# Running the first layer of a fused attention and two-layer kernel in two passes of eight feature chunks

## The chip, the cores and the metric

The kernel runs on one core of a Trainium2 chip. The metric is the device time of one launch in microseconds (us). Engines are named as the profile names them: PE is TensorE (matmuls), PEld its weight loads, DVE is VectorE, ACT is ScalarE, POOL is GpSimd, SP is the engine whose queue issues every DMA of this kernel.

## What is computed

Three steps follow each other on 3072 tokens: an attention over chunks of 32 queries with a short window, then `h * cos(h)` between two products, then a maximum of three products and a last product. The weights come as float64.

```python
for c in range(768 // 32):                       # 4 batches, 8 heads of 64
    k_full = concat([mem_k, k[c*32-16 : c*32+40]])   # 8 memory keys, 16 left, 8 right
    a = softmax(q_c @ k_full.T / 8)
    out_c = a @ v_full
x = out.reshape(3072, 512)
h = x @ w_in                                     # 512 -> 2048
x = (h * cos(h)) @ w_out                         # 2048 -> 512
h = maximum(maximum(x @ w1, x @ w2), x @ w3)     # 512 -> 768
y = h @ w_out2                                   # 768 -> 512
```

## The kernel before

**Blocks, slots, products.** The 3072 tokens are 8 blocks of 384 (`NBLK`, `N`). The 2048 features of the first layer are 16 chunks of 128 (`FA`). One block with one chunk is a *slot*; slots are numbered through all blocks, so before the change slot 16 is block 1, chunk 0. Every product is done in three passes, because each operand is split into a high and a low float32r part. A slot has a first product, `p1` (12 matmuls into `h`, L319), a *chain* on the other engines, and a second product, `p2` (12 matmuls into four accumulators `acc`, L348). `LOOK = 2`: the program writes `p2` of slot s-2 behind `p1` of slot s.

**The chain of a slot** makes `g = h cos h`: ScalarE `ki` (L328), VectorE L330 and L331, ScalarE sine (L333), VectorE L335, ScalarE high part of `g` (L337), GpSimd low part of `g` (L338). So a slot takes three VectorE instructions.

**Weight decoding.** A weight tile (128x512 float64, 512 KB) is loaded, has its exponent rebased (`w_exp`: one instruction on GpSimd, L154, or ScalarE, L152, and one on ScalarE, L156), takes two integer instructions on VectorE (`w_bits`: L161 and L163, called its first and its second half here), is copied to its high part by ScalarE (`w_hi`, L169), and gets its low part by a subtraction (`w_lo`, L174) on GpSimd for the first layer, and in turns on VectorE and GpSimd for the second. The first layer has 32 tiles, the second 24. A loaded tile sits in a staging tile until its low part is made. Before the change there are 9 staging tiles in the first layer, 6 in the second. `Decode` takes up two tiles in a slot (`RATE`) in the first layer, about 1.1 in the second.

**Attention.** A block has 3 *duos* of 128 queries. The tables `FIRST`, `SECOND` and `STEADY` say after which slot a step of a later duo is written: S scores on TensorE (L208), with two additions of the mask and a maximum on VectorE (L223, L228) and a subtraction on GpSimd (L229); E one exponential for a block (L233); N a sum, an addition and a reciprocal on VectorE (L238, L239, L240) and a multiplication on GpSimd (L241); T transposes (L250), evicted half by ScalarE, half by VectorE (L254); V values (L266), evicted by ScalarE and VectorE (L270, L271). The attention of block 0 is done ahead of the slots.

**Stages.** A start with loads, the attention of block 0 and the first two tiles; 16 slots of block 0 beside the other 30 tiles and the attention of block 1; six blocks with attention alone; block 7, without attention, beside the 24 tiles of the second layer; then the second layer, 48 steps of `b3` (L395) and `b4` (L416). The output of the first layer goes to DRAM (`x2d`) and comes back block by block (`b_dma`, `b_conv`).

**What sets the order.** The program is written as above, but the order in which instructions stand in each engine's queue is made when the program is built, by a list scheduler of the kernel language. It may put an instruction ahead of earlier written ones as soon as its tiles have a free buffer and its inputs exist. Each engine then takes its queue strictly in that order.

Of the kernel before, what the change touches and what calls it, by code (L numbers as in the profile page):

```python
# [41 lines left out]
LOOK = 2  # slots that a second product waits for its operand  # L42

# Emission plan. A slot is one of the FA feature chunks of a token block; it names the steps of the attention of later
# duos that follow its products: S scores, E exponential of a whole block, N normalization, T transposes, V values.
# [21 lines left out]
def attn_moe_kernel(ctx, tc, qT, kT, vw, w_in, w_out, w3, w2o, out):  # L67
# [56 lines left out]
    stage_state = {}  # L124

    def stage_open(keys, n_raw, n_tmp):
        """Staging tiles; the first n_raw of them hold the last weights in the end."""
        tiles = [wp.tile([128, 512, 2], I32, tag="w", name=f"raw{i}") for i in range(n_raw)]
        tiles += [tmp["pool"].tile([128, 512, 2], I32, name=f"wst{i}", bufs=1) for i in range(n_tmp)]
# [545 lines left out]
```

## Time and profile before

| | before |
|---|---|
| time, median of 3 runs | 1098.11 us (1097.15 to 1098.32) |
| span of the profiled execution | 1098.8 us |
| TensorE busy, matmuls | 1056.0 us, 96% |
| VectorE busy | 513.2 us, 47% |
| ScalarE busy | 433.6 us, 39% |
| GpSimd busy | 316.1 us, 29% |

The span is taken from the first to the last instruction of one profiled execution; it is 0.7 us above the median of the timed runs. Shares are means over stages that differ: the stages have to be read one by one.

### The profile page before, as it was taken

The numbers are of one execution on the slowest core, as the hardware profiler recorded it, in microseconds if no ns is written. First come the engines' busy times: TensorE is split into PE (matmuls) and PEld (weight loads), VectorE is DVE, ScalarE is ACT, GpSimd is POOL, SyncE is SP. The second block draws the span as 40 slices with busy tenths as digits, with TensorE's granted clock in tenths as the row PEclk, the third lists the DMA queues.
The fourth block names the chain that finished last, engine by engine and source line by source line (L and its number), as shares of the span: only waits on it lengthen the run. The fifth ranks groups of instructions, "written<-read, shape, count | busy, mean of one in ns | idle before, by whom it ended". The sixth has DMA issues, their size and how long they took to land.

```text
span 1098.8 us, 17081 instructions
## 1 busy us (share of the span) xinstructions
PE 1056.0 (96%) x6989; PEld 1003.9 (91%) x6989; DVE 513.2 (47%) x913; ACT 433.6 (39%) x811; POOL 316.1 (29%) x267
## 2 busy tenths in 40 slices
PE   8768899999999999999999988999999999999998
PEld 5667899999999999999999887999999999999997
DVE  5999856546346355454433998312221221222121
ACT  5667645535445335435444887211111121211111
POOL 2887635324224224233222445210101010101000
PEclk8989999999999999999999989999999999999999
DMA  9744213011111012101101662101101000100000
GB/s 287 248 150 134 83 63 97 30 65 59 30 51 58 30 52 72 44 23 30 44 16 39 226 204 78 58 5 53 30 29 30 29 29 30 58 1 30 1 30 29
DMA packets 28111, 72.94 MB, mean 66 GB/s; under 512 B 3200, under 2 KB 7296, under 8 KB 28032
## 3 DMA queue, kind: packets, MB, share of 16 engines
q1 hardware_dynamic: 28032, 71.84, 20.2%
q8 instruction: 55, 0.90, 0.3%
q14 instruction: 24, 0.20, 0.1%
HBM read 59.24 MB, written 12.58 MB: 65 GB/s over the span
## 4 chain that ended last, share of the span: by engine, by line
PE 80%; DVE 10%; issue 4%; ACT 2%; DMA 2%; POOL 1%; SPq 0%; DVEq 0%; POOLq 0%; ACTq 0%
PE h L395 27%; PE acc L348 19%; PE h L319 18%; PE acc L416 9%; PE s L208 3%; PE s L266 2%; DVE raw L161 2%; PE s L250 2%; DVE ki L331 2%; DVE wst L161 2%; DVE raw L163 1%; DVE wst L163 1%; DVE ki L330 1%; DVE ki L335 1%; DMA wst<-in_w_in_dram 1%
## 5 line engine op out<-in xcount | busy, mean ns | idle before, releaser
L319 PE MATMUL h<-x,w 128*128 128x384 f32 x1536 | 296.9, 341 | 20.2 <-DVE ki L335 15.8
L348 PE MATMUL acc<-g,w 128*128 128x384 f32 x1536 | 298.2, 341 | 12.3 <-POOL g L338 10.6
L395 PE MATMUL h<-x,w 128*128 128x384 f32 x1728 | 308.2, 335 | 0.0
L395 PEld LDWEIGHTS h<-x,w 128*128 128x128 f32 x1728 | 302.0, 188 | 4.0
L319 PEld LDWEIGHTS h<-x,w 128*128 128x128 f32 x1536 | 272.3, 191 | 25.6 <-DVE ki L335 17.9
L348 PEld LDWEIGHTS acc<-g,w 128*128 128x128 f32 x1536 | 268.2, 190 | 17.7 <-POOL g L338 13.2
L338 POOL TENSOR_TENSOR g<-ki,g 128x384 fp32r<-128x384 f32 x128 | 136.7, 1068 | 323.4 <-ACT g L337 269.1
L330 DVE SCALAR_TENSOR_TENSOR ki<-h,ki 128x384 f32<-128x384 f32 x128 | 70.9, 554 | 166.7 <-ACT ki L328 166.7
L402 DVE TENSOR_TENSOR r<-h,r 128x384 f32<-128x384 f32 x48 | 26.7, 557 | 210.3 <-PE h L395 210.3
L333 ACT ACTIVATE ki<-ki,pio 128x384 f32<-128x384 f32 x128 | 78.9, 616 | 106.3 <-DVE ki L331 106.0
L377 POOL TENSOR_TENSOR x<-xs,x 128x384 fp32r<-128x384 f32 x31 | 33.8, 1118 | 273.8 <-ACT x L376 273.8
L416 PE MATMUL acc<-w,g 128*128 128x512 f32 x432 | 107.3, 393 | 0.0
L328 ACT ACTIVATE ki<-h 128x384 int32<-128x384 f32 x128 | 62.3, 487 | 109.7 <-PE h L319 109.5
L335 DVE TENSOR_TENSOR ki<-h,ki 128x384 f32<-128x384 f32 x128 | 70.5, 551 | 54.6 <-ACT ki L333 54.4
L337 ACT ACTIVATE g<-ki 128x384 fp32r<-128x384 f32 x128 | 67.1, 525 | 72.2 <-DVE ki L335 72.1
L405 ACT ACTIVATE g<-r 128x384 fp32r<-128x384 f32 x48 | 25.1, 522 | 176.5 <-DVE r L403 176.5
L416 PEld LDWEIGHTS acc<-w,g 128*128 128x128 f32 x432 | 80.4, 188 | 14.7
L401 ACT ACTIVATE r<-h 128x384 f32<-128x384 f32 x48 | 23.6, 492 | 130.4 <-PE h L395 130.3
L331 DVE TENSOR_SCALAR ki<-ki 128x384 f32<-128x384 f32 x128 | 61.0, 477 | 2.7
L403 DVE TENSOR_TENSOR r<-h,r 128x384 f32<-128x384 f32 x48 | 26.7, 557 | 69.4 <-PE h L395 69.4
L208 PEld LDWEIGHTS s<-k,q 64*64 64x64 f32 x768 | 34.4, 137 | 8.7 <-issue 6.4
L406 DVE TENSOR_TENSOR g<-r,g 128x384 fp32r<-128x384 f32 x48 | 27.4, 571 | 31.1 <-ACT g L405 31.1
(72 smaller groups left out, 775.6 us busy)
## 6 DMA issues: line engine op xcount, KB each, us to landing
v<-in_vw_dram SPq DMA_DIRECT2D x24, 384.0 KB, 3.4
wst<-in_w_dram SPq DMA_DIRECT2D x18, 512.0 KB, 3.8
k<-in_kT_dram SPq DMA_DIRECT2D x24, 320.0 KB, 3.4
q<-in_qT_dram SPq DMA_DIRECT2D x24, 256.0 KB, 2.8
x2d<-x SPq DMA_DIRECT2D x32, 192.0 KB, 1.9
xs<-x2d SPq DMA_DIRECT2D x16, 384.0 KB, 3.1
out_dram<-ost SPq DMA_DIRECT2D x24, 256.0 KB, 2.0
raw<-in_w_out_dram SPq DMA_DIRECT2D x11, 512.0 KB, 5.8
```

Source lines behind the costliest of these rows:

```text
L208: PE.matmul(p[p0:p0 + 64, hh, :], lhsT=q[p0:p0 + 64, t, hh, :], rhs=k[p0:p0 + 64, hh, QU * t:QU * t + KU], start=first, stop=first or hh == 3)
L319: PE.matmul(h, lhsT=w[:, a, 128 * k:128 * k + 128], rhs=x[:, b, k, :], start=(n == 0), stop=(n == 11))
L328: ACT.activation(out=ki, in_=h, func=AF.Copy, scale=INV2PI, bias=0.25)
L330: DVE.scalar_tensor_tensor(c, h, INV2PI, ki, op0=ALU.mult, op1=ALU.subtract)
L331: DVE.tensor_scalar(c, c, -0.75, 0.25, op0=ALU.max, op1=ALU.min)
L333: ACT.activation(out=c, in_=c, func=AF.Sin, scale=2 * math.pi, bias=pio2)
L335: DVE.tensor_tensor(c, h, c, op=ALU.mult)
L337: ACT.activation(out=g[:, 0, :], in_=c, func=AF.Copy)
L338: POOL.tensor_tensor(g[:, 1, :], c, g[:, 0, :].bitcast(F32), op=ALU.subtract)
L348: PE.matmul(acc[j][m][:, :N], lhsT=w[:, a, 128 * m:128 * m + 128], rhs=g[:, b, :], start=(f == 0 and n == 0), stop=(f == FA - 1 and n == 2))
L395: PE.matmul(h, lhsT=w[:, a, 128 * k:128 * k + 128], rhs=x[:, b, k, :], start=(n == 0), stop=(n == 11))
L416: PE.matmul(o[m], lhsT=g[:, a, 128 * m:128 * m + 128], rhs=w[:, b, :], start=(f == 0 and n == 0), stop=(f == FB - 1 and n == 2))
```

## The change

Block and chunk change places in part. The first pass runs chunks 0 to 7 over all eight blocks, the second pass chunks 8 to 15 over all eight blocks (`slots`). So slot 8 is now block 1, chunk 0, and a block has 8 slots in a pass. Everything else follows from that:

- All attention lies in the first pass, 3 duos in 8 slots. `SECOND` also writes the scores of the next block a block early, and `X` the exponential two blocks ahead.
- `x` of every block is stored to DRAM (`x_store`, 1.5 MB) and loaded again for the second pass (`x_load`).
- Each pass leaves its own sums: `x2d` is double, `b_dma` loads both, `b_conv` adds them with one VectorE instruction for each half (128x768).
- There are no staging tiles: a loaded weight tile takes a buffer of the pool `wp` (32 buffers), like decoded weights. `live` counts them as the program is written, and `load` stops at 8 tiles ahead, or when fewer than 3 buffers are left.
- `goal` sets how many tiles are to be taken up by a slot: 2 for a slot up to the first 16, the other 16 spread over the rest of the first pass, 3 in 10 slots of the second layer's in the second pass, and 2 for a slot in its last block.

```diff
-FIRST = {0: "S0", 1: "S1", 2: "S2", 3: "E", 5: "N0", 6: "N1 T0", 7: "V0", 9: "T1", 10: "V1", 11: "N2", 12: "T2", 13: "V2"}
-STEADY = {1: "E", 3: "S3", 4: "N0 N1 T0", 6: "S4 S5", 7: "N2 V0 T1", 11: "V1", 13: "T2", 14: "V2"}
+F1 = 8
+FIRST = {0: "S0", 1: "S1", 2: "S2 E", 4: "N0 N1 N2", 5: "T0", 6: "V0 T1 V1", 7: "T2 V2"}
+STEADY = {0: "N0 N1 S3", 1: "N2", 2: "T0 S4", 3: "V0 T1", 4: "V1 S5", 5: "T2 V2", 7: "X"}
...
-NRAW, NTMP, NTMPB = 7, 2, 6
-RATE, RATEB = 2, 1.1
+NW, NAHEAD = 32, 8
+RATE = 2
...
-        t = stage(key)
+        t = wp.tile([128, 512, 2], I32, tag="w", name="raw")
+        live[0] += 1
...
+    def x_store(j):
+        SP.dma_start(out=xd[j], in_=xT[j].bitcast(F32))
+
+    def x_load(j):
+        x = xT[1, j] = xp.tile([128, 2, 4, N], F32R, tag="x", name="x")
+        SP.dma_start(out=x.bitcast(F32), in_=xd[j])
...
-        x, t = xT[NBLK + j], xs.pop((j, g))
+        x, (t, u) = xT[NBLK + j], xs.pop((j, g))
+        DVE.tensor_tensor(t, t, u, op=ALU.add)
...
+    keysA = keys_of(0, F1) + keys_of(F1, FA)
...
-            while n > 0 and self.nl < len(self.keys) and stage_state["prev"][self.keys[self.nl]] < self.ns:
+            while n > 0 and self.nl < len(self.keys) and self.nl - self.ns < NAHEAD and live[0] + 3 <= NW:
...
+    slots = [(0, j, f) for j in range(NBLK) for f in range(F1)]
+    slots += [(1, j, f) for j in range(NBLK) for f in range(F1, FA)]
+    total, half = len(slots), NBLK * F1
+
+    def goal(s):
+        if dec.keys is keysB:
+            return (s - half) * 3 // 10 if s < total - FA + F1 else dec.nb + 2
+        lead = 2 + RATE * (s + 1)
+        return lead if lead <= 2 * F1 else 2 * F1 + (s - F1 + 1) * 2 * (FA - F1) // (half - F1 - 4)
...
-        decoding = s < FA + 2 or j == NBLK - 1
-        if decoding:
-            dec.begin(RATE if s < FA + 2 else max(0, min(2, int(RATEB * (f + 1)) - dec.nb)))
+        dec.begin(max(0, min(2, goal(s) - dec.nb)))
```

The order of two queues moves with it. First VectorE, where the decoding of the first layer ends. Before, these are the last tiles (in the staging tiles `wst0` and `wst1`) and the slots behind them; L161 and L163 are the two halves, L330, L331 and L335 the chain:

```order
L161 SCALAR_TENSOR_TENSOR wst0_106<-wst0_106 128x512
L163 SCALAR_TENSOR_TENSOR wst0_106<-wst0_106 128x512
L161 SCALAR_TENSOR_TENSOR wst1_107<-wst1_107 128x512
L163 SCALAR_TENSOR_TENSOR wst1_107<-wst1_107 128x512
L330 SCALAR_TENSOR_TENSOR ki_1336<-h_1323,ki_1336 128x384
L331 TENSOR_SCALAR ki_1336<-ki_1336 128x384
L335 TENSOR_TENSOR ki_1336<-h_1323,ki_1336 128x384
L330 SCALAR_TENSOR_TENSOR ki_1380<-h_1367,ki_1380 128x384
L331 TENSOR_SCALAR ki_1380<-ki_1380 128x384
L335 TENSOR_TENSOR ki_1380<-h_1367,ki_1380 128x384
```

In the changed program (whose line numbers differ: L149 and L151 are the halves, L335, L336 and L340 the chain, L215 and L220 the mask and maximum of a duo, L246 and L264 evictions) this is VectorE in slot 14, that is block 1, chunk 6. `raw_4107` and `raw_4147` are tiles 31 and 32 of the first layer, which the program writes in slots 56 and 57:

```order
L335 SCALAR_TENSOR_TENSOR ki_1495<-h_1482,ki_1495 128x384
L336 TENSOR_SCALAR ki_1495<-ki_1495 128x384
L264 TENSOR_TENSOR x_1435<-s_1508,x_1435 128x4x128
L340 TENSOR_TENSOR ki_1495<-h_1482,ki_1495 128x384
L149 SCALAR_TENSOR_TENSOR raw_4107<-raw_4107 128x512
L215 TENSOR_TENSOR sm_1271<-s_1541,maskb_86 128x384
L151 SCALAR_TENSOR_TENSOR raw_4107<-raw_4107 128x512
L215 TENSOR_TENSOR sm_1271<-s_1542,maskb_86 128x384
L149 SCALAR_TENSOR_TENSOR raw_4147<-raw_4147 128x512
L220 TENSOR_REDUCE mx_1565<-sm_1271 128x8
L246 COPY pt_1568<-s_1575 96x512
L151 SCALAR_TENSOR_TENSOR raw_4147<-raw_4147 128x512
```

So in VectorE's queue all 32 tiles of the first layer are decoded by slot 14 in the changed program, as by slot 13 before; between them now stands the attention of two blocks.

Second TensorE's queue around the fifth `p1`. Before it goes on in turn (`h` is a `p1`, four rows of `acc` a `p2`); these are `p1` of slot 4, `p2` of slot 2, `p1` of slot 5, `p2` of slot 3:

```order
L319 MATMUL h<-x,w 128x384 x12
L348 MATMUL acc_616<-g,w 128x384 x3
L348 MATMUL acc_617<-g,w 128x384 x3
L348 MATMUL acc_618<-g,w 128x384 x3
L348 MATMUL acc_619<-g,w 128x384 x3
L319 MATMUL h<-x,w 128x384 x12
L348 MATMUL acc_616<-g,w 128x384 x3
```

In the changed program (L316 is `p1`, L354 `p2`, L242 the transposes of a duo) `p2` of slot 2 stands ahead of `p1` of slot 4, and transposes stand between:

```order
L354 MATMUL acc_637<-g,w 128x384
L354 MATMUL acc_638<-g,w 128x384
L354 MATMUL acc_639<-g,w 128x384 x3
L354 MATMUL acc_640<-g,w 128x384 x3
L242 MATMUL s<-ident,sm 96x128
L316 MATMUL h<-x,w 128x384 x2
L242 MATMUL s<-ident,sm 96x128 x4
L316 MATMUL h<-x,w 128x384 x12
L242 MATMUL s<-ident,sm 96x128 x3
L354 MATMUL acc_637<-g,w 128x384 x2
```

The transposes, which need the normalized duo from GpSimd, moved in front of the rest of `p1` of slots 4 and 5.

## Rows read from the trace of the kernel before

**Rows 1.** Windows (us): busy time of each engine, granted clock of TensorE, DMA.

```profile
31.60:138.46 106.86, 84.60 (x576) 77.50 (x576) 101.88 (x126) 70.69 (x124) 84.75 (x60) 0.92 0.46 150
39.80:136.20 96.40, 75.95 (x518) 69.98 (x517) 92.19 (x117) 64.71 (x114) 75.25 (x53) 0.93 0.44 145
138.46:606.23 467.77, 467.76 (x3600) 455.57 (x3601) 224.99 (x447) 209.53 (x360) 150.89 (x133) 1.00 0.15 49
606.23:689.08 82.85, 73.24 (x386) 69.50 (x385) 78.12 (x111) 65.92 (x126) 42.01 (x32) 0.96 0.48 159
689.08:1098.70 409.62, 404.80 (x2185) 385.74 (x2184) 87.81 (x156) 69.32 (x141) 29.65 (x29) 1.00 0.09 30
```

**Rows 2.** Timeline of TensorE: where `p1` of some slots starts.

```profile
322.74 2.24 PE L319 MATMUL h<-x,w 128*128 128x384 f32 x12
326.90 2.24 PE L319 MATMUL h<-x,w 128*128 128x384 f32 x12
334.16 2.36 PE L319 MATMUL h<-x,w 128*128 128x384 f32 x12
...
284.74 2.24 PE L319 MATMUL h<-x,w 128*128 128x384 f32 x12
289.78 1.03 PE L319 MATMUL h<-x,w 128*128 128x384 f32 x5
...
353.05 2.24 PE L319 MATMUL h<-x,w 128*128 128x384 f32 x12
358.50 0.68 PE L319 MATMUL h<-x,w 128*128 128x384 f32 x3
```

**Rows 3.** VectorE's groups, 40 to 140 us: busy us, mean ns | idle before.

```profile
L163 DVE SCALAR_TENSOR_TENSOR raw<-raw 128x512 int32<-128x512 int32 x18 | 18.9, 1054 | 0.2
L161 DVE SCALAR_TENSOR_TENSOR raw<-raw 128x512 int32<-128x512 int32 x16 | 18.5, 1162 | 0.0
L331 DVE TENSOR_SCALAR ki<-ki 128x384 f32<-128x384 f32 x15 | 13.0, 868 | 0.1
L163 DVE SCALAR_TENSOR_TENSOR wst<-wst 128x512 int32<-128x512 int32 x8 | 11.9, 1490 | 0.1
L330 DVE SCALAR_TENSOR_TENSOR ki<-h,ki 128x384 f32<-128x384 f32 x16 | 8.7, 546 | 2.1 <-ACT ki L328 2.1
...
L161 DVE SCALAR_TENSOR_TENSOR wst<-wst 128x512 int32<-128x512 int32 x8 | 6.4, 804 | 1.6 <-ACT wst L156 1.6
L223 DVE TENSOR_TENSOR sm<-s,maskb 128x384 f32<-128x384 f32 x6 | 3.2, 543 | 0.0
L228 DVE TENSOR_REDUCE mx<-sm 128x8 f32<-128x768 f32 x3 | 2.8, 939 | 0.0
...
L239 DVE TENSOR_SCALAR rs<-rs 128x8 f32<-128x8 f32 x3 | 2.3, 804 | 0.0
L254 DVE COPY pt<-s 96x512 f32<-96x512 f32 x3 | 2.0, 678 | 0.0
```

**Rows 4.** Single lines: duration in ns, least/median/most; the first in 450 to 550 us.

```profile
L331 DVE TENSOR_SCALAR ki<-ki x21: 346/359/361, 454.5 to 549.1; 128x384 f32<-128x384 f32 x21
...
L161 DVE SCALAR_TENSOR_TENSOR raw<-raw x22: 674/1226/1955, 26.0 to 123.6; 128x512 int32<-128x512 int32 x22
...
L174 POOL TENSOR_TENSOR w<-raw,w x22: 1299/1740/2104, 33.1 to 128.8; 128x512 fp32r<-128x512 f32 x22
...
L229 POOL TENSOR_TENSOR sm<-sm,mx x21: 1469/1470/1914, 43.3 to 492.2; 128x768 f32<-128x768 f32 x21
...
L338 POOL TENSOR_TENSOR g<-ki,g x128: 994/1014/1518, 46.6 to 692.2; 128x384 fp32r<-128x384 f32 x128
```

**Rows 5.** VectorE's groups, 600 to 700 us: the halves of the second layer's tiles.

```profile
L163 DVE SCALAR_TENSOR_TENSOR wst<-wst 128x512 int32<-128x512 int32 x24 | 22.9, 952 | 0.2
L161 DVE SCALAR_TENSOR_TENSOR wst<-wst 128x512 int32<-128x512 int32 x24 | 21.1, 878 | 3.5 <-ACT wst L156 3.2
```

**Rows 6.** The page's DMA issues: count, KB each, us to landing.

```profile
raw<-in_w_out_dram SPq DMA_DIRECT2D x11, 512.0 KB, 5.8
```

More of the change, by code (lines that the diff above doesn't have):

```diff
@@ L95, in attn_moe_kernel @@
     pio2 = const.tile([128, 1], F32, name="pio2")
-    x2d = [dp.tile([128, 4, N], F32, name=f"x2d{j}") for j in range(NBLK)]
+    x2d = [[dp.tile([128, 4, N], F32, name=f"x2d{p}{j}") for j in range(NBLK)] for p in range(2)]
+    xd = [dp.tile([128, 2, 4, N], F32, name=f"xd{j}") for j in range(NBLK)]
+    live = [0]
     def constants():
@@ L122, in attn_moe_kernel @@
     DST = {"in": wA_in, "out": wA_out, "b": wB, "bo": wB_out}
[L124 to L129, printed above, removed]
-        last = [len(keys) - n_raw + i if i < n_raw else len(keys) for i in range(n_raw + n_tmp)]
-        used = [-1] * len(tiles)
-        plan, prev = {}, {}
-        for n, key in enumerate(keys):
-            i = min((i for i in range(len(tiles)) if n < last[i]), key=lambda i: (used[i], -last[i]))
-            plan[key], prev[key], used[i] = tiles[i], used[i], n
-        stage_state["plan"], stage_state["prev"] = plan, prev
-    def stage(key):
-        return stage_state["plan"][key]
     def w_load(key):
@@ L217, in a_add @@
         if d % DB == 0:
-            p = tmp["pool"] if d // DB > 1 and d // DB % 2 else t2
+            p = tmp["pool"] if d // DB % 2 else t2
             sm3[d // DB] = p.tile([128, DB, 2, 4, KU], F32, tag="sm", name="sm", bufs=1)
@@ L257, in a_v @@
         p, v = pt[d], vt[d]
+        live[0] -= d < DB and ts[-1] == 1
         j, o = divmod(d, DB)
@@ L365, in b_dma @@
         for g in range(2):
-            t = tmp["pool"].tile([128, 2, N], F32, tag="xs", name="xs")
-            SP.dma_start(out=t, in_=x2d[j][:, 2 * g:2 * g + 2, :])
-            xs[j, g] = t
+            xs[j, g] = []
+            for ps in range(2):
+                t = tmp["pool"].tile([128, 2, N], F32, tag=f"xs{ps}", name="xs")
+                SP.dma_start(out=t, in_=x2d[ps][j][:, 2 * g:2 * g + 2, :])
+                xs[j, g].append(t)
     def b_conv(j, g):
@@ L426, in b4, with keys_of @@
                 SP.dma_start(out=out[r0:r0 + 128, :], in_=t)
-    keysA = [("in", 0)]
-    for f in range(1, FA):
-        keysA += [("in", f), ("out", f - 1)]
-    keysA.append(("out", FA - 1))
+    def keys_of(f0, f1):
+        keys = [("in", f0)]
+        for f in range(f0 + 1, f1):
+            keys += [("in", f), ("out", f - 1)]
+        return keys + [("out", f1 - 1)]
+    keysA = keys_of(0, F1) + keys_of(F1, FA)
     keysB = []
@@ L580, in slot @@
         do2()
+        if ps == 0 and f == 1:
+            x_store(j)
+        if f == (F1 if ps else F1 - 2) and (ps or j == NBLK - 1) and (not ps or j + 1 < NBLK):
+            x_load(j + 1 if ps else 0)
     for s in range(total):
-        if s == FA + 2:
-            tmp_close()
-            tmp_open("sm2", 1)
-        if s == total - FA:
+        if s == half:
             tmp_close()
```

86 lines of the change are left out of this document (49 added, 37 removed).

## The prediction

> **What bounds the kernel now.** I read the windows first, by stage [rows 1]. The stages are cut where `p1` of slot 0, of slot 16, of slot 112 and the first product of the second layer start. In the six blocks from 138.46 us on TensorE is busy for 467.76 of 467.77 us at the full clock (1.00 granted, the 2.4 GHz level), and in the second layer for all but 5 of 410 us. In the two stages that decode, 31.60 to 138.46 and 606.23 to 689.08 us, it is busy for 79% and 88% only, while VectorE is busy for 95% and 94%. There VectorE is the bound.
>
> What a slot costs when TensorE is the bound comes from its timeline [rows 2]: a plain slot 4.16 us (322.74 to 326.90); with two duos' scores 7.26, so 1.55 for a duo; with one duo's transposes 5.04, so 0.88; with one duo's values 5.45, so 1.29. A duo takes 3.72 us of TensorE. The 128 slots and 21 duos of the first layer need 128 x 4.16 + 21 x 3.72 = 610.6 us. From 31.60 to 689.08 us they took 657.5. So 46.9 us are lost, and by stage:
>
> - block 0: 106.86 - (16 x 4.16 + 3 x 3.72 = 77.7) = 29.2 us;
> - six blocks: 467.77 - (96 x 4.16 + 18 x 3.72 = 466.3) = 1.5 us;
> - block 7: 82.85 - 66.6 = 16.3 us.
>
> No rearrangement of the first layer can give more than these 46.9 us. The second layer and the start keep their work.
>
> **The first stage after the change.** The `goal` of the change spreads tiles 17 to 32 over the first pass, but the scheduler's order does not: in VectorE's queue all 32 tiles are decoded by slot 14, as the piece of order shows. An engine takes its queue in order, so what counts is VectorE's work up to there. Its prices are means of that stage [rows 3]: first half of a tile (18.5 + 6.4) / 24 = 1.04 us, second half (18.9 + 11.9) / 26 = 1.19; a chain 0.546 + 0.868 + 0.546 = 1.96 (L335 priced like L330); an addition of the mask 0.543, a maximum 0.939 (a sum the same), L239 0.804, an eviction 0.678, a reciprocal 0.2 by estimate.
>
> Before, slots 0 to 13 hold 14 chains, 24 first and 26 second halves and the attention of 3 duos: 27.4 + 55.9 + 16.0 = 99.3 us, against 96.4 us of time from 39.80 to 136.20 us, the chains of slots 0 and 14 [rows 1]. Records overlap a little, so a microsecond of these rows is worth 0.971.
>
> After, I count in VectorE's queue from the chain of slot 0 to that of slot 16: 16 chains 31.4; 25 first and 26 second halves 56.9; 18 additions, 9 maxima, 9 sums, 9 L239, 9 reciprocals, 12 evictions of attention 43.8; two evictions of `acc` 1.1. Together 133.2, by 0.971 129.3 us. The start keeps its loads and their order, so the chain of slot 0 stays at 39.8 and that of slot 16 comes at 169.1; its `p1` ends some 0.5 us before, at 168.6. Until then TensorE's queue holds 17 `p1` and 15 `p2` (32 x 2.08 = 66.6), and 9.5 duos' scores, 6 duos' transposes and values (27.7): 94.3 us. The loss is 168.6 - 31.6 - 94.3 = 42.7 us in place of 29.2: **13.5 us more**. The reason in a sentence: the decoding stays as dense, and each duo that now lies beside it needs 5.2 us of VectorE (16.0 / 3, by 0.971) for 3.72 us of TensorE.
>
> Two things could move this. The end below is 5 us, from the first rival. The end above is 17: the sums wait for the exponential of a whole block, and that falls into this stretch three times, before once. TensorE's queue also has `p2` of slot 2 and transposes ahead of `p1` of slot 4, so its lead over VectorE is smaller. I take 13.5, since in that stage VectorE was busy for 92.2 of 96.4 us [rows 1], and so its own time is the nearest row.
>
> **A rule against this sum.** The integer halves take 0.674 us at least, 1.226 in the middle and 1.955 at most; L331 takes 0.359 in the middle of a quiet stretch and 0.868 on average in this stage [rows 3, 4]. VectorE is not slower there: it waits inside its instructions while GpSimd works. The Trainium skill says why ("SBUF — State Buffer", Who interferes with whom): VectorE and GpSimd share a port pair under an exclusive lock, held for a whole instruction. The trace agrees, with 0.36 against 0.87 us for the same instruction. By that rule the wait is not a property of VectorE's instruction, and pricing attention steps that don't use the pair beside it could be too dear. What the sum would be then, worked out from rows, is the first rival, 8.4 us lower.
>
> **Steady blocks of the first pass.** A block has 8 x 4.16 + 3 x 3.72 = 44.4 us of TensorE, and VectorE 8 chains, 3 duos and an eviction, about 32 us by these rows. TensorE's queue keeps its two slots of lead there. Before, six such blocks lost 1.5 us; I add 0.5, bounds 0 and 3.
>
> **The decoding of the second layer.** It moves from one place to two. In VectorE's queue 16 tiles stand in slots 57 to 69 (the last block of the first pass and the first of the second), and none in 70 to 120, where the pool is full. The other eight are finished in slots 121 to 126, once the last block frees buffers. By [rows 5] a half costs 0.88 or 0.95 us, a low part on VectorE about 0.9 (as a half).
>
> - Before: slots 110 to 124 hold 24 tiles: 15 chains 29.4, 43.9 for the halves, 12 low parts 10.6, evictions and the like 2.3, 86.2 us, against 15 x 4.16 + 1.29 = 63.7 of TensorE. The overrun of 22.5 cost 16.3 us: two slots of lead absorb a part.
> - After, slots 57 to 69: 25.5 + 29.3 + 7 x 0.88 + 2.2 = 63.2 against 54.1, overrun 9.1.
> - After, slots 120 to 126: 13.7 + 14.6 + 5 x 0.88 + 1.1 + two additions of halves at 1.1 by estimate (1.5 times a half's least time) = 36.0 against 29.1, overrun 6.9.
>
> If the overrun costs in proportion (16.3 / 22.5), that is 11.6 us; if a fixed 6.2 us is absorbed in each place, 3.6. I take 6.5, nearer to the second, since the lead is a matter of slots. So **9.8 us less** than the 16.3 before. Bounds: 2 and 14; the upper one has loads that come late, below.
>
> **What costs nothing, and its cover.** Storing and loading `x` moves 8 x 1.5 MB each way, the second `x2d` 6 MB each way. DMA is busy for 15% in the six blocks [rows 1]. A load of 512 KB lands in 5.8 us in the busy start [rows 6], so 1.5 MB by some 18 us, and it is issued a block (33 us) ahead. Without that cover a block would wait up to 18 us. The store of block 0 stands on SP's queue ahead of later tiles' loads, which are several tiles ahead of VectorE. The 14 additions of halves in the second layer, 1.1 us each, lie beside a VectorE that is busy for 87.8 of 409.6 us. Without that, they would be 15 us.
>
> **Sum.** 1098.8 + 13.5 + 0.5 - 9.8 = 1103.0 us of span; the median of the runs lay 0.7 below the span, so **1102.3**.
>
> **Rivals.**
> 1. *The pair that VectorE and GpSimd use in turn is the bound, not VectorE; then the change is faster.* Least durations [rows 4]: halves 0.675, L331 0.346, GpSimd's L174 1.3, L229 and L241 1.47, L338 1.0, L154 0.65 by estimate (half of L174). Before, in slots 0 to 13: VectorE's part 50 x 0.675 + 14 x 0.346 + 0.5 = 39.1, GpSimd's 14 + 25 x 1.3 + 6 x 0.65 + 5 x 1.47 = 57.8: 96.9 for 96.4 us of time, which speaks strongly for it. After, in slots 0 to 15: 41.3 + 16 + 26 x 1.3 + 3.9 + 18 x 1.47 = 121.5, by the same ratio 120.9. The stage then loses 8.4 us less than in my sum: 1093.9. It decides if attention's other VectorE work truly runs beside GpSimd. Against it: in slots 8 to 15 scores, exponential, normalization, transposes and values hang on each other within few slots.
> 2. *The last eight loads come late.* Each can be issued only when a `p1` or `p2` of the last block frees a buffer, and 5.8 us to landing [rows 6] is more than a slot; ScalarE would stand before the exponent, and the chain behind it. One microsecond in each of the slots 121 to 127: 1110.
> 3. *The two stages cancel.* With 9 in place of 13.5, half way to the first rival: 1098, no change.
> 4. *The change does what `goal` says*, 16 tiles fewer in the first stage: 16 x 2.23 x 0.971 = 35 us less of VectorE there, about 1070. The order in the queue speaks against it.
>
> **How the numbers follow.** I give 0.45 to the forecast (1100.5 to 1107), 0.2 to the first rival, 0.12 to the second, 0.2 to the third, 0.03 to the fourth. 0.2% is 2.2 us, about what a measurement can tell here, since three runs spread over 1.2 us. Faster is the first and fourth, 0.23; same the third, 0.2; slower the forecast and the second, 0.57. The range 1092 to 1111 leaves out the fourth rival and the ends where both bounds fall together. For slower alone it is 1100.5 to 1111.
>
> **What would show it.** Right: the chain of slot 16 at 165 to 172 us; VectorE over 90% busy until there; `p1` of slots 17 to 56 without gaps; two shallow dips of TensorE, at the change of pass and at the end of the second pass, of about 4 and 3 us; the second layer as long as before, 409.6 us. Wrong: a chain of slot 16 near 160 us, dips that are deep, waits of ScalarE on `raw` loads, or of TensorE on the loaded `x`.

## The result and the profile after

| | before | after |
|---|---|---|
| device time, median of 4 runs | 1098.21 us (1097.15 to 1099.02) | 1108.05 us (1106.72 to 1109.58) |
| ratio to before, 95% interval | | 1.0078 [1.0055, 1.0100] |
| span of the profiled execution | 1098.8 us | 1106.8 us |
| first product of slot 0 | 31.60 us | 31.22 us |
| lost up to slot 55 (before: blocks 0 to 6) | 30.7 us | 40.6 us |
| lost from there to the second layer | 16.3 us | 13.8 us |
| second layer | 409.6 us | 410.6 us |

The change makes the kernel 9.8 us slower. The forecast was 4.2 us slower, 1102.3 us. "Lost" is the time beyond what TensorE needs by [rows 2], counted by whole slots: 4.16 us a slot and 3.72 a duo.

The windows of the changed kernel, cut where `p1` of slots 0, 16, 56, 72 and 120 and the first product of the second layer start, answer to [rows 1]: start and end, microseconds, busy time of TensorE, its weight load, VectorE, ScalarE and GpSimd, granted clock, DMA share, GB/s.

```profile
31.22:164.44 133.22, 107.96 (x916) 96.65 (x916) 115.68 (x168) 86.01 (x140) 95.50 (x68) 0.90 0.54 184
164.44:382.90 218.46, 217.58 (x1916) 206.19 (x1917) 123.91 (x237) 101.87 (x172) 80.34 (x67) 1.00 0.33 117
382.90:460.03 77.13, 70.76 (x386) 67.87 (x386) 58.06 (x89) 52.39 (x100) 30.60 (x24) 0.98 0.50 174
460.03:659.71 199.68, 199.68 (x1154) 199.68 (x1154) 79.15 (x160) 85.18 (x160) 51.10 (x50) 1.00 0.22 78
659.71:696.20 36.49, 34.05 (x194) 33.15 (x193) 30.90 (x47) 26.61 (x50) 16.22 (x14) 1.00 0.57 181
696.20:1106.80 410.60, 405.43 (x2185) 385.60 (x2184) 100.78 (x172) 71.54 (x147) 32.99 (x31) 1.00 0.12 39
```

Slots 0 to 15 need 16 x 4.16 + 9 x 1.55 + 6 x 2.17 = 93.5 us (nine duos' scores, six duos' transposes and values), took 133.2, and so lose 39.7. The next 40 slots lose 0.9, slots 56 to 71 lose 77.1 - 66.6 = 10.6, slots 72 to 119 nothing, and the last eight 3.2.

VectorE is busy for 87% of the first row. Its groups there answer to [rows 3]: count, busy time, mean of one in ns, idle time before them.

```profile
L151 DVE SCALAR_TENSOR_TENSOR raw<-raw 128x512 int32<-128x512 int32 x28 | 31.5, 1134 | 0.1
L149 DVE SCALAR_TENSOR_TENSOR raw<-raw 128x512 int32<-128x512 int32 x28 | 27.1, 974 | 7.8 <-ACT raw L144 5.4 <-POOL raw L142 1.8 <-issue 0.5
L336 DVE TENSOR_SCALAR ki<-ki 128x384 f32<-128x384 f32 x16 | 11.6, 724 | 0.1
```

What TensorE waited for in that row is mixed. The list of its waits (sum, times, longest) begins:

```profile
PE h L316 <- POOL w L163: 5.7, 3, 4.5
PE acc L354 <- ACT w L158: 5.4, 1, 5.4
PE s L242 <- POOL sm L233: 3.5, 1, 3.5
PE h L316 <- DVE ki L340: 3.4, 2, 1.8
```

GpSimd's low part of a weight (L163) and its attention step (L233) are there, ScalarE's high part (L158), and VectorE's chain (L340) only fourth. Before the change that chain was the first by far, 14.9 of the 22.3 us that TensorE idled from slot 0 to slot 16. The same list of the kernel before begins:

```profile
PE h L319 <- DVE ki L335: 14.9, 5, 6.6
```

After the change TensorE idles for 133.2 - 108.0 = 25.3 us in this stage. The other 14.4 of the 39.7 us are products that ran slower. TensorE's timeline shows where, a wait in brackets:

```profile
60.87 4.31 PE L354 MATMUL acc<-g,w 128*128 128x384 f32 x12 [5.43 <-ACT w L158]
...
74.96 3.57 PE L316 MATMUL h<-x,w 128*128 128x384 f32 x10 [4.49 <-POOL w L163]
...
80.39 2.24 PE L316 MATMUL h<-x,w 128*128 128x384 f32 x12
```

Twelve products take 2.24 us at the full clock and 4.31 us after the wait of 5.43: about the ratio of the two levels, 2.4 and 1.2 GHz. The granted clock was 0.50 from 60.87 to 65.00 us and from 74.96 to 78.30, and 1.00 in the products at 80.39. The stage's granted clock is 0.90 on average.

The unexpected loss lies in slots 56 to 71, the last block of the first pass and the first of the second. There the decoding of the second layer begins, in buffers that the last block of the first pass sets free. The timeline of several engines (start, duration, engine, line; a wait in brackets):

```profile
390.45 1.01 SPq L133 DMA_DIRECT2D raw<-in_w_dram  x2
...
394.40 0.67 ACT L140 ACTIVATE raw<-raw 128x512 f32<-128x512 f32 x1 [1.97 <-DMA raw<-in_w_dram]
394.97 0.64 ACT L144 ACTIVATE raw<-raw 128x512 int32<-128x512 uint16 x1
...
395.69 0.69 DVE L149 SCALAR_TENSOR_TENSOR raw<-raw 128x512 int32<-128x512 int32 x1 [2.67 <-ACT raw L144]
...
396.42 1.38 DVE L151 SCALAR_TENSOR_TENSOR raw<-raw 128x512 int32<-128x512 int32 x1
...
397.73 0.54 DVE L363 COPY x<-acc 128x384 f32<-128x384 f32 x1
...
398.33 0.79 PE L354 MATMUL acc<-g,w 128*128 128x384 f32 x3 [3.30 <-DVE x L363]
...
398.96 3.26 PE L316 MATMUL h<-x,w 128*128 128x384 f32 x12
```

Read it from the top. A load is issued at 390.45, into a buffer just freed. ScalarE's queue has its exponent next and waits until it lands. VectorE's queue has the two halves of that tile ahead of the second eviction of an accumulator, so the eviction of a sum that TensorE had finished at 391.4 comes at 397.73. This is the sum of the block before, and the next block's first products into that accumulator wait 3.30 us for it; the next `p1` takes 3.26 us in place of 2.24. Of the 10.6 us, TensorE idled for 6.4: 4.3 for evictions by VectorE (L363), 1.9 for GpSimd's low part of `g` (L343), 0.2 for an eviction by ScalarE. The rest are slower products. Six loads of this line, issued from 390.5 to 404.9, landed in (microseconds):

```profile
DMA to landing us min/median/max: 3.4/3.7/5.4
```

### The profile page after: what moved, and what is told of

Same layout as the page of the kernel before. It is cut to its first block, busy times and chain, and to the rows that moved or that the text cites. A ratio compares the mean times of both kernels' runs of the same rounds, so it can differ in the third digit from the quotient of the medians.

```text
span 1106.8 us, 17286 instructions
## 1 busy us (share of the span) xinstructions
PE 1060.1 (96%) x6989; PEld 1004.0 (91%) x6989; DVE 529.7 (48%) x945; ACT 440.9 (40%) x827; POOL 315.4 (28%) x267
## 3 DMA queue, kind: packets, MB, share of 16 engines
q1 hardware_dynamic: 37248, 109.59, 29.2%
## 4 chain that ended last, share of the span: by engine, by line
PE 74%; DVE 3%; issue 2%; DMA 2%; ACT 2%; POOL 1%; DVEq 0%; POOLq 0%; ACTq 0%
PE h L405 26%; PE h L316 17%; PE acc L354 17%; PE acc L426 9%; PE s L259 2%; PE s L200 1%; PE s L242 1%; DMA raw<-in_w_dram 1%; DMA xs<-x2d 1%; DVE raw L151 1%; DVE ki L336 1%; POOL x L387 1%; DVE raw L149 1%; POOL g L343 0%; DMA x2d<-x 0%
## 5 line engine op out<-in xcount | busy, mean ns | idle before, releaser
L354 PE MATMUL acc<-g,w 128*128 128x384 f32 x1536 | 302.8, 342 | 14.9 <-DVE x L363 5.5
L316 PE MATMUL h<-x,w 128*128 128x384 f32 x1536 | 298.5, 342 | 9.7 <-POOL w L163 5.7
L354 PEld LDWEIGHTS acc<-g,w 128*128 128x128 f32 x1536 | 270.4, 191 | 21.2 <-POOL g L343 6.5
L316 PEld LDWEIGHTS h<-x,w 128*128 128x128 f32 x1536 | 271.9, 191 | 14.2 <-POOL w L163 6.5
L343 POOL TENSOR_TENSOR g<-ki,g 128x384 fp32r<-128x384 f32 x128 | 139.2, 1087 | 302.1 <-ACT g L342 228.4
L335 DVE SCALAR_TENSOR_TENSOR ki<-h,ki 128x384 f32<-128x384 f32 x128 | 71.0, 554 | 151.2 <-ACT ki L333 150.6
L333 ACT ACTIVATE ki<-h 128x384 int32<-128x384 f32 x128 | 62.3, 487 | 113.2 <-PE h L316 99.0
L340 DVE TENSOR_TENSOR ki<-h,ki 128x384 f32<-128x384 f32 x128 | 70.7, 552 | 59.8 <-ACT ki L338 59.6
L163 POOL TENSOR_TENSOR w<-raw,w 128x512 fp32r<-128x512 f32 x44 | 68.6, 1565 | 34.5 <-ACT w L158 34.5
L336 DVE TENSOR_SCALAR ki<-ki 128x384 f32<-128x384 f32 x128 | 61.1, 477 | 2.5
L151 DVE SCALAR_TENSOR_TENSOR raw<-raw 128x512 int32<-128x512 int32 x56 | 59.3, 1063 | 0.4
L413 DVE TENSOR_TENSOR r<-h,r 128x384 f32<-128x384 f32 x48 | 26.8, 558 | 60.7 <-PE h L405 60.1
```

The lines of the kernel that those rows point to most:

```text
L151: DVE.scalar_tensor_tensor(lw, hw, SIGN, lw, op0=ALU.bitwise_and, op1=ALU.bitwise_or)
L163: eng.tensor_tensor(w[:, 1, :], wst.pop(key)[:, :, 0].bitcast(F32), w[:, 0, :].bitcast(F32), op=ALU.subtract)
L316: PE.matmul(h, lhsT=w[:, a, 128 * k:128 * k + 128], rhs=x[:, b, k, :], start=(n == 0), stop=(n == 11))
L335: DVE.scalar_tensor_tensor(c, h, INV2PI, ki, op0=ALU.mult, op1=ALU.subtract)
L336: DVE.tensor_scalar(c, c, -0.75, 0.25, op0=ALU.max, op1=ALU.min)
L340: DVE.tensor_tensor(c, h, c, op=ALU.mult)
```

## The experiments

Each run starts from the changed kernel and is compared with the kernel before: the median, then the ratio with its 95% interval; where no interval stands, there was one execution. The kernel before took 1100.1 to 1100.7 us beside these runs, 2 us more than in the table, so the ratios are what can be compared. Stages are cut at `p1` of a slot, each in one profiled execution. Line numbers shift by some lines between the kernels; the names stay.

**Loads of the second pass's tiles held back.** The order of the queues ignores `goal`, so a data dependence enforces it: a loaded buffer first takes one column from the `g` of the slot where the load was written, and three tiles at most are under way.

```diff
+        if gate_src and GATED(key):
+            POOL.tensor_copy(t[:, 0:1, 0].bitcast(F32), gate_src[-1][:, 0, 0:1].bitcast(F32))
         SP.dma_start(out=t.rearrange("p c t -> p (c t)"), in_=src.bitcast(I32))
...
-            while n > 0 and self.nl < len(self.keys) and self.nl - self.ns < NAHEAD and live[0] + 3 <= NW:
+            while n > 0 and self.nl < len(self.keys) and self.nl - self.ns < (3 if gate_src and GATED(self.keys[self.nl]) else NAHEAD) and live[0] + 3 <= NW:
```

> Before the load of each of the 16 weight tiles of the second pass a one-element copy of a g tile into the raw tile, and at most three of them in flight, so that the order built has 20 of the 32 tiles decoded by slot 10 and the rest spread over slots 11 to 46. If VectorE's own work sets the first 16 slots (my step A), 11 tiles of 2.2 us on VectorE leave them: from p1 of slot 0 to p1 of slot 16 it takes 107 to 113 us in place of 133.2, slots 16 to 56 stay at 218 to 222 us, and the whole is 1083 to 1090 us. If the first stage is instead set by late loads or by GpSimd's chain of low parts and subtractions, the stretch stays above 122 us and the whole above 1097 us. Slots 56 to 72 keep their 77 us either way.

Measured: 1105.84 us, 1.0056 [1.0039, 1.0073]. Slots 0 to 15 took 120.0 us, not 107 to 113, and slots 16 to 55 229.4, not 218 to 222. Of the 13.2 us gained in the first stage, 10.9 are given back in the next; some 2 us of both are TensorE's own work, which moved behind the cut (893 products in the first window, 916 in the kernel as changed). All of the gain lies in slots 8 to 15: 53.3 us in place of 66.7, with the first halves of 3 tiles in place of 12. Slots 0 to 7 took 66.6 us (66.5 in the kernel as changed). VectorE is busy for 95.3 of the 120.0 us, 79%: so VectorE's sum is not its measure. The stage lies between the two expectations, the whole on the rival's side. By the whole it is not clear that this is faster than the kernel as changed, whose interval overlaps.

**Loads of the second layer's tiles held back.** The same edit for the other tiles.

> The same hold, put on the tiles of the second layer alone: 5 tiles decoded in slots 57 to 63 and 11 in slots 71 to 103, where 16 stood in slots 57 to 69. If the 10.6 us lost in slots 56 to 72 come from second evictions and products that stand behind decoding which waits for its loads (theory C), the stretch from p1 of slot 56 to p1 of slot 72 falls from 77.1 to 69 to 73 us, slots 72 to 120 stay without a gap, and the whole is 1100 to 1104 us. If the loss belongs to the change of pass itself (eviction, GpSimd's g), the stretch stays above 75 us and the whole at 1106 to 1109 us.

Measured: 1113.32 us, 1.0127 [1.0107, 1.0147]. The windows from `p1` of slot 56 on to that of slot 72, and on to where `p1` of slot 112 starts:

```profile
380.30:446.80 66.50, 66.50 (x385) 66.50 (x384) 31.14 (x59) 33.62 (x64) 20.93 (x23) 1.00 0.30 104
446.80:623.30 176.50, 170.16 (x962) 165.96 (x961) 89.17 (x161) 84.27 (x163) 52.48 (x56) 1.00 0.31 106
```

TensorE is busy throughout the first row. VectorE takes 4 first halves there, not 16: with most of the decoding out of it, the stretch loses nothing, where it lost 10.6 us. So the loss comes from the decoding and not from the change of pass itself, as theory C has it. But 40 slots behind it, which need 166.4 us, now take 176.5, and the last eight 42.9 in place of 36.5. The list of waits of the second row says why:

```profile
DVE raw L156 <- ACT raw L151: 18.0, 7, 3.6
ACT raw L147 <- DMA raw<-in_w_dram: 14.0, 8, 2.5
...
PE acc L362 <- DVE x L371: 3.8, 4, 1.2
```

It is the same chain as before at every block's end: a load held back lands late, ScalarE and VectorE stand before it, and the eviction stands behind them. The hold moved the late loads; it did not make them early.

**Both holds.**

> Both holds together. If the two losses are apart, the gains add up: 1075 to 1086 us, below the kernel before the change. If one loss only moves into the other stage, it is no better than the better of the two alone.

Measured: 1110.64 us, 1.0093 [1.0067, 1.0120], no better than the first hold alone. The losses had moved: slots 56 to 71 took 68.6 us, slots 72 to 119 206.9 in place of 199.7, the last eight 41.6.

**Evictions taken off VectorE.**

```diff
-                if m % 2 == 0:
-                    ACT.activation(out=t, in_=acc[ps, j][m][:, :N], func=AF.Copy)
-                else:
-                    DVE.tensor_copy(t, acc[ps, j][m][:, :N])
+                ACT.activation(out=t, in_=acc[ps, j][m][:, :N], func=AF.Copy)
```

> All four evictions of an accumulator on ScalarE, decoding untouched. If VectorE's queue in slot 57 is what holds the second product (theory C), TensorE's wait of 3.3 and 1.0 us for the eviction goes and slots 56 to 72 take 72 to 74 us, the whole 1103 to 1105 us. If ScalarE's queue is as late, because it is the one that waits for the raw tiles, the stretch stays at 76 to 79 us and the whole at 1107 to 1110 us.

Measured: 1103.73 us, 1.0040 [1.0027, 1.0054]. Slots 56 to 71 took 77.5 us: no change there, as the rival had it. The timeline at the same place:

```profile
393.78 0.65 ACT L140 ACTIVATE raw<-raw 128x512 f32<-128x512 f32 x1 [2.67 <-DMA raw<-in_w_dram]
...
395.95 0.49 ACT L360 ACTIVATE x<-acc 128x384 f32<-128x384 f32 x1 [0.56 <-POOL g L343]
...
396.50 0.79 PE L354 MATMUL acc<-g,w 128*128 128x384 f32 x3 [3.01 <-ACT x L360]
```

The wait has only changed its name. ScalarE's queue holds the same late tile ahead of the eviction. The whole, though, lies where the first expectation had it (1103 to 1105 us), some 4 us below the kernel as changed by the two ratios. The profiled execution was the slowest of ten runs (1107.54 us), so where these 4 us come from is not shown.

**Work taken off VectorE, off GpSimd, and off both.** The first leaves out the sign bit of the first layer's weights, the second their low parts (TensorE multiplies high parts in their place).

```diff
-            self.ops = [(k, i) for i in range(2) for k in self.cur]
+            self.ops = [(k, i) for i in range(1 if self.keys is keysA else 2) for k in self.cur]
```

> Leaves out the sign bit of the 32 weight tiles of the first layer, which takes one of the two halves of each tile (about 1.1 us) off VectorE and nothing off GpSimd. Of the 32, 26 stand behind the start of slot 0. If VectorE's sum sets the first 16 slots (step A), they take 104 to 112 us in place of 133.2, a VectorE still over 85% busy or the stretch near TensorE's own 93.5 us. If GpSimd's queue (exponents, low parts, two attention steps a duo, g) sets them, they take 122 to 133 us, with VectorE under 75% busy.

```diff
-        eng.tensor_tensor(w[:, 1, :], wst.pop(key)[:, :, 0].bitcast(F32), w[:, 0, :].bitcast(F32), op=ALU.subtract)
+        t = wst.pop(key)
+        if key[0] not in ("in", "out"):
+            eng.tensor_tensor(w[:, 1, :], t[:, :, 0].bitcast(F32), w[:, 0, :].bitcast(F32), op=ALU.subtract)
...
-                PE.matmul(h, lhsT=w[:, a, 128 * k:128 * k + 128], rhs=x[:, b, k, :],
+                PE.matmul(h, lhsT=w[:, 0, 128 * k:128 * k + 128], rhs=x[:, b, k, :],
...
```

> Leaves out the low parts of the 32 weight tiles of the first layer (TensorE multiplies the high part in their place, as many products as before), which takes 32 subtractions of about 1.5 us off GpSimd and nothing off VectorE. By VectorE's sum with durations as they are: 127 to 133 us for the first 16 slots. If the two engines hold each other up (rival 1 of the prediction), VectorE's halves shrink from 1.0 and 1.2 us towards 0.7 and the stretch falls to 112 to 120 us. If GpSimd's queue itself is what comes last, the stretch falls to 112 to 120 us too, but with the halves' durations as they were and VectorE above 90% busy or waiting for something else.

> Leaves out both the sign bit and the low parts of the first layer's weights. Alone, the first took 31.5 us of VectorE's work out of the first 16 slots and gave 7.9 us of the 133.2, the second 46.8 us of GpSimd's and gave 16.2. If each engine's queue has its own places where it comes last, the gains add up: 107 to 111 us. If they hide each other (whichever is left still sets the stage), both together give more than the sum: 96 to 104 us, near TensorE's own 93.5. If what is left is neither, but the order of dependent steps and TensorE's clock after its waits, the stretch stays above 112 us.

Measured: 1100.60, 1085.02 and 1075.48 us. The first 16 slots without the sign bit:

```profile
30.03:155.33 125.30, 105.22 (x896) 94.27 (x896) 84.63 (x135) 85.31 (x140) 85.61 (x67) 0.92 0.59 200
```

without the low parts:

```profile
28.07:145.07 117.00, 104.36 (x916) 95.09 (x916) 105.19 (x168) 85.91 (x140) 49.94 (x39) 0.91 0.62 214
```

and without both:

```profile
28.50:134.90 106.40, 98.25 (x896) 89.51 (x897) 77.68 (x132) 83.19 (x139) 46.03 (x38) 0.96 0.66 235
```

31.1 us less of VectorE's busy time shortened the stage by 7.9 us, and left VectorE 68% busy, as the second expectation had it. So VectorE's sum did not set it. (Some 1.6 of the 7.9 us are TensorE's work behind the cut: 896 products, not 916.) 45.6 us less of GpSimd shortened it by 16.2. Together they gave 26.8, close to 7.9 + 16.2, and the stage's 106.4 us lie just under the 107 to 111 expected of gains that add up: each queue has places of its own where it comes last. Each of the three is one execution. And without the low parts VectorE's busy time fell by 10.5 us, though none of its instructions had been taken away. Its groups in that run:

```profile
L151 DVE SCALAR_TENSOR_TENSOR raw<-raw 128x512 int32<-128x512 int32 x28 | 27.5, 991 | 0.1
L149 DVE SCALAR_TENSOR_TENSOR raw<-raw 128x512 int32<-128x512 int32 x28 | 23.9, 860 | 2.1 <-ACT raw L144 2.0
...
L338 DVE TENSOR_SCALAR ki<-ki 128x384 f32<-128x384 f32 x16 | 8.7, 546 | 0.1
```

The same 28 and 28 halves went from 1134 and 974 ns to 991 and 860, the chain's clamp from 724 to 546. Part of VectorE's "busy" time had been waiting for GpSimd, as the first rival said. It goes the other way too: without the sign bit, GpSimd's low parts went from 1624 ns on average to 1407, though none of them had changed. The Trainium skill ("SBUF — State Buffer", Who interferes with whom) has this as an exclusive lock on a shared port pair, which reductions never use. The trace agrees: the maxima kept 0.94 us in either run.

**Exponents of the first 16 tiles on ScalarE.**

```diff
-POOL_EXP = 16
+POOL_EXP = 0
```

> The exponents of the first 16 tiles on ScalarE (0.67 us each) in place of GpSimd (0.9 us): some 9 us less on GpSimd in slots 0 to 8, some 7 us more on ScalarE, which is 60% busy there. If GpSimd's backlog is what TensorE waits for there (5.7 us on low parts in slots 3 to 5), slots 0 to 8 fall from 66.5 to 58 to 63 us and the whole to 1100 to 1104 us. If VectorE's sum sets them, no change: 65 to 68 us, 1106 to 1110 us.

Measured: 1101.73 us, 1.0014 [1.0001, 1.0027]. The whole is in the range expected of GpSimd's backlog. The profiled execution was again the slowest of ten (1105.50 us), and in it the gain does not lie where it was expected: slots 0 to 7 took 66.2 us, unchanged, and slots 8 to 15 61.8 in place of 66.7. GpSimd was relieved (85.7 us busy, 95.5 before). In slots 0 to 7 TensorE idled for 11.6 us in place of 15.7, but at a granted clock of 0.82 in place of 0.85 and with one more `p2`. So this profile does not tell where the gain of the median lies.

**The decoding held back, the load not.** The scale of the first decoding step is read from a column that GpSimd writes from `g`.

```diff
+                scale = gsc[:, len(gates):len(gates) + 1]
+                gates.append(scale)
+                POOL.tensor_scalar(scale, gate_src[-1][:, 0, 0:1].bitcast(F32), 0.0, 2.0 ** -112, op0=ALU.mult, op1=ALU.add)
+            ACT.activation(out=hw, in_=hw, func=AF.Copy, scale=scale)
```

> Holds back the decoding and not the load: the scale of the first decoding step of the 16 tiles of the second pass and of the first 16 of the second layer is read from a column that GpSimd writes from the g of the slot meant, while their loads run ahead as in the kernel as changed. Slots 0 to 16 should take about 120 us, as with the load held back, but if the loss of the earlier holds in slots 16 to 56 (10.9 us) and 72 to 112 (11 us) came from steps that stood in VectorE's and ScalarE's queues for a load still under way, it goes: slots 16 to 56 at 218 to 222 us, 56 to 72 at 66.6 to 69 us, 72 to 120 at 199.7 to 202 us, and the whole 1082 to 1092 us, below the kernel before. If decoding itself, spread over the slots, costs TensorE those microseconds, the stretches stay at 229 and 211 us and the whole at 1103 to 1110 us.

Measured: 1099.22 us, 0.9985 [0.9972, 0.9998], by the two ratios about 10 us less than the kernel as changed, but not the 1082 to 1092 that were expected. The windows from `p1` of slots 0, 16, 56 and 72:

```profile
30.00:152.30 122.30, 104.75 (x917) 93.81 (x917) 93.27 (x143) 71.74 (x114) 74.79 (x62) 0.92 0.54 184
152.30:378.30 226.00, 219.98 (x1916) 206.05 (x1917) 145.88 (x257) 116.07 (x197) 95.25 (x87) 1.00 0.36 123
378.30:445.50 67.20, 66.91 (x386) 66.50 (x385) 32.45 (x64) 38.76 (x74) 21.10 (x24) 1.00 0.44 158
445.50:645.60 200.10, 199.96 (x1154) 199.64 (x1153) 94.94 (x185) 98.24 (x186) 60.17 (x66) 1.00 0.26 91
```

The second pass is as expected: 16 tiles decoded between slots 57 and 105 now cost 0.6 + 0.4 us, where they cost 10.6 as changed, packed into slots 58 to 70, and over 10 with the loads held back. With loads that have landed, decoding spread like this is nearly free. VectorE and ScalarE still stood before these steps from slot 56 to slot 119, 36.5 and 19.6 us in all, since the column from GpSimd lets them go one by one; for a load ScalarE stood only 1.6. So standing by itself did not cost TensorE time here; it does when an eviction stands behind it, as in the timeline of the kernel as changed. In the first pass the decoding is not free: slots 16 to 55 still lose 226.0 - 217.6 = 8.4 us. TensorE waits there mostly for evictions of attention, 4.2 us for ScalarE's (L255, L274) and 1.8 for VectorE's (L275). And the end pays: the last eight slots took 38.0 us in place of 36.5, and the second layer 414.0 in place of 410.6, with one wait of 2.6 us for the chain's VectorE step (L351) near its start.

**The 16 tiles of the second pass in slots 6 and 7 of a block.** `goal` then rises only there, by three tiles a block.

```diff
-        return lead if lead <= 2 * F1 else 2 * F1 + (s - F1 + 1) * 2 * (FA - F1) // (half - F1 - 4)
+        if lead <= 2 * F1:
+            return lead
+        j, f = divmod(s, F1)
+        return 2 * F1 + (0 if j == 0 else [0, 3, 6, 9, 12, 14, 16, 16, 16][j - (f < 6)] - (f == 6 and j < 7))
```

> The decoding held back as before, and the 16 tiles of the second pass put into slots 6 and 7 of the blocks 1 to 6, where no scores, normalization or transposes stand. With the tiles spread evenly, slots 16 to 56 took 226.0 us in place of 218.5. If decoding costs there because it stands in a queue ahead of evictions of attention that TensorE waits for, the stretch goes back to 218.5 to 221 us and the whole falls by 4 to 7 us, to 1092 to 1095 us. If any decoding in these blocks costs TensorE time, it stays at 224 to 228 us, 1097 to 1100 us.

Measured: 1105.17 us, 1.0046 [1.0028, 1.0065]: the wrong way. Slots 16 to 55 took 230.0 us. VectorE's queue shows three tiles on end in slots 32 and 33, where a block begins; L346 and L351 are the chain's first and last step:

```profile
246.62 0.56 DVE L346 SCALAR_TENSOR_TENSOR ki<-h,ki 128x384 f32<-128x384 f32 x1 [0.86 <-ACT ki L344]
...
249.43 1.36 DVE L160 SCALAR_TENSOR_TENSOR raw<-raw 128x512 int32<-128x512 int32 x2 [1.84 <-ACT raw L151]
250.71 0.55 DVE L351 TENSOR_TENSOR ki<-h,ki 128x384 f32<-128x384 f32 x1
251.17 1.28 DVE L162 SCALAR_TENSOR_TENSOR raw<-raw 128x512 int32<-128x512 int32 x2
254.30 1.01 DVE L160 SCALAR_TENSOR_TENSOR raw<-raw 128x512 int32<-128x512 int32 x1 [1.84 <-ACT raw L151]
255.23 0.55 DVE L346 SCALAR_TENSOR_TENSOR ki<-h,ki 128x384 f32<-128x384 f32 x1
```

It stood twice for 1.84 us before ScalarE, and the next slot's chain (L346) came at 255.23, 8.6 us after the one ahead of it. That is more than the two slots of 4.16 us by which TensorE leads, and two slots later TensorE waits:

```profile
259.06 2.37 PE L327 MATMUL h<-x,w 128*128 128x384 f32 x12 [1.53 <-DVE ki L351]
```

A row of tiles costs more than the same tiles spread. The idea behind the placing was right in part: TensorE's waits for evictions of attention in slots 16 to 55 fell from 6.0 us to 1.9, but it now waited 5.2 us for the chain (L351) and 2.8 for evictions of accumulators.

**With the exponents on ScalarE, and with a thinner second block.** The first adds `POOL_EXP = 0` to the run above; the second, in addition, gives blocks 0 and 1 the plan `FIRST` and block 2 `SECOND`.

> As the run with the tiles in slots 6 and 7, and the exponents of the first 16 tiles on ScalarE. If GpSimd's backlog in the first block is a separate cause, the gain of 5 to 6 us that this gave to the kernel as changed comes on top: 1086 to 1090 us. If holding back the tiles has already taken that backlog away: 0 to 2 us on top, 1091 to 1095 us.

> As the run before it, and the second block does only its three duos (the plan of the first block for both; the scores ahead of time begin a block later). Three duos' scores, 6 us of VectorE and 5 us of GpSimd, leave slots 8 to 16. If attention beside the decoding is what the first stage loses time on (the sentence of step A), the first pass up to slot 56 loses 2 to 5 us less than in the run before: 1083 to 1088 us. If the loss lies in slots 0 to 8 alone, no change: within 1.5 us of the run before.

Measured: 1102.15 us, 1.0010 [0.9990, 1.0030], and 1098.30 us, 0.9988 [0.9971, 1.0005]. The exponents gave 0.36% of the time, 4 us: between the two expectations, nearer to a gain of its own, but the intervals just overlap. In the profile of the first, the second fastest of ten runs, slots 0 to 7 took 62.3 us, in place of 66.0 with the exponents on GpSimd: there, at least, some of the gain lies where it was expected. Both wholes lie far above what was expected, since the placement they stand on cost time. The thinner block moved the ratio by 0.2%, 2.4 us, in its theory's direction, but the intervals overlap, and the profile of the second (the slowest of ten runs) needed 350.1 us from slot 0 to slot 56 against 348.2. Slots 8 to 15 took 46.2 us in place of 55.7, and the 40 slots behind them 9.5 us more: the scores moved with their cost. Whether attention beside decoding is what costs is not settled by it.

No version that does all of the work beats the kernel before by more than 0.2%. The best is the held decoding with tiles spread evenly. With exponents on ScalarE that version was not run.

## Why the prediction held, and where it did not

**First stage: the time was close, and that was luck.** The chain of slot 16 was put at 169.1 us and came at 168.34. The stage from the chain of slot 0 to that of slot 16 answers to [rows 1]:

```profile
36.77:168.34 131.57, 106.20 (x907) 95.11 (x903) 115.88 (x168) 85.69 (x140) 95.02 (x68) 0.91 0.53 185
```

VectorE's work up to there was summed to 129.3 us and took 115.9. It idled for the other 15.7, which the sum put at nothing. And the chain of slot 0 came at 36.77, 3.0 us before the 39.8 taken from the kernel before. The three errors cancel. So the step "its own time is the nearest row" failed: 31.1 us less of VectorE's time gave 7.9, and VectorE fell to 68% while the stage stayed long. Its share was 87%, not over 90%. What the runs show in its place: TensorE waits for GpSimd, ScalarE and VectorE in turn, 25.3 us in all, and loses 14.4 us more on products at the lower clock after these waits. Keeping 16 tiles out of the stage took 11 us off slots 8 to 15 and nothing off slots 0 to 7, so the decoding there is a cause in the later half; whether it needs the attention beside it, and how the loss of the earlier half divides among the queues, is not shown.

**The 13.5 us set two counts against each other.** The 29.2 of before are counted by 16 whole slots, the 42.7 of after by the products in TensorE's queue, 17 `p1` and 15 `p2`. These are the groups of `p2` from `p1` of slot 0 to that of slot 16, first before, then after:

```profile
L348 PE MATMUL acc<-g,w 128*128 128x384 f32 x168 | 32.7, 341 | 2.7 <-POOL g L338 2.7
L354 PE MATMUL acc<-g,w 128*128 128x384 f32 x180 | 40.4, 372 | 5.9 <-ACT w L158 5.4 <-POOL g L343 0.5
```

Twelve products make a `p2`: 14 stood there before, 15 after. Counted by products, the stage before lost 106.9 - (30 x 2.08 + 11.2) = 33.3 us. So the step comes to 9.4 and the whole sum to 1098.2 us, which is the third rival's "no change". That the forecast said slower rests on this slip of 4.1 us. Measured by products, the stage lost 41.0 us after the change, 7.7 more; by whole slots it lost 39.7, which is 10.5 more.

**Rival 1** was right in its mechanism and wrong in its time. VectorE's instructions are lengthened by GpSimd (10.5 us in this stage, by its low parts alone), but that pair is not the bound either: from the chain of slot 0 to that of slot 16 it gave 120.9 us, and 131.6 were measured.

**Rival 4**, a `goal` that takes effect, was priced at 35 us. With real holds the first stage gave 10.9 to 13.2, and 7.5 to 10.9 came back in slots 16 to 55. VectorE's price for a tile was the wrong measure here too.

**Steady blocks:** 2.0 us were forecast and 0.9 lost by whole slots, 3.8 by products, inside the bounds given.

**The change of pass is the mis-sized term.** Both places of second-layer decoding were forecast to lose 6.5 us (about 4 and 3) in place of 16.3; they lost 10.6 and 3.2. So 2.5 us were gained, not 9.8: the 13.8 us lost lie at the upper bound of 14, which had been set for loads that come late. These 7.3 us are most of the way from the recounted sum, no change, to the slower kernel that was measured. The step compared VectorE's work with TensorE's (63.2 against 54.1 us), as if the queue were always supplied. Loads that were issued when a buffer came free put ScalarE and VectorE to waiting, with an accumulator's eviction behind them. Two of the signs named for a wrong prediction appeared with it: a deep dip, and 4.5 us of ScalarE waiting for `raw` loads. That the decoding is the cause is shown: with three quarters of it elsewhere the stretch loses nothing (66.5 us). That the late loads are a part of it is shown by the timeline and by the two holds: spread over slots 72 to 119, the tiles lost 10.1 us with the loads held back and 0.4 with the decoding held back. Moving the eviction to another engine did not help (77.5 us, TensorE waiting 3.01 for ScalarE). No run packs the 16 tiles as densely with their loads landed, so how much of the 10.6 us is the dense decoding itself stays open. The second rival saw late loads, but only for the last eight tiles, where they did little.

**What costs nothing** nearly held: the second layer took 410.6 us in place of 409.6, and TensorE never waited for a loaded `x`, of which the first three loads landed in 6.1 to 6.6 us, not in some 18.

**The sum.** Between the two profiled executions, by whole slots: start -0.4, first stage +10.5, steady blocks -0.6, second-layer decoding -2.5, second layer +1.0, together 8.0 us against 4.2. The rest of the 9.8 is the step from a span to a time. The runs of the changed kernel take 1.8 us beyond their span, and later runs of the kernel before about 2.0 (1098.46 us with a span of 1096.4). By these 2.0 the profiled execution of before, with its span of 1098.8, took some 1100.8 us, more than any of the four timed runs: the 0.7 taken off came from a slower execution. The 1108.05 us lie above the 1100.5 to 1107 of the forecast proper, inside the wider range, and near the second rival's 1110 without its reason.

## What to carry to other kernels

A busy share does not make an engine the bound. Here VectorE was busy for 87% of a stage and 31.1 us less of its time gave 7.9: part of that time its instructions were lengthened by GpSimd, and TensorE mostly waited for others. Look first at the durations of one instruction in and out of the stage, then at what the waiting engine names. In a queue that is taken in order, a step whose load was still under way delayed everything behind it: here it was better to hold back the decoding than the load, and to spread the tiles, since a row of three cost more than the lead of two slots covers. The pacing rule of this program did nothing where the scheduler ordered the queues, until a dependence carried it. And when a stage is compared with another, count the work in both by the same rule.

## What the runs showed of the hardware

- Some waits of TensorE are paid for twice. After waits of 5.43 and 4.49 us the products took 4.31 us for twelve and 3.57 for ten at a granted clock of 0.50, against 2.24 for twelve at full clock; over the first stage slower products are 14.4 us beside 25.3 us of waiting.
- The runs of one kernel differ along with the granted clock: with the exponents on ScalarE, the ten runs go from 1099.08 us at 0.990 to 1105.50 us at 0.981. Slots 0 to 7 of that last execution took 66.2 us at 0.82; in another kernel with the same exponents they took 62.3 at 0.92. One profile of such a kernel may lie 4 us from its median, so a difference of that size in the first stage of a single profile carries little. The start varies too: in seven kernels whose start is written alike, slot 0 began between 28.0 and 31.4 us.
- VectorE's clamp of a 128x384 tile took 724 ns on average beside GpSimd's low parts and 546 without them, its integer halves 1134 and 974 against 991 and 860 ns; the chain's first instruction (544 and 546) and the maxima (941 and 942) did not change.
